# Twelve unread matrix products ahead of the first attention steps of a one-core retention and feed-forward kernel

## The chip, the cores and the metric

The kernel runs on one core of one Trainium2 chip. The metric is device microseconds (us) of one execution. The three runs of the kernel before have a median of 849.66 us, from 848.78 to 849.99.

## The reference

A retention layer with a decaying state, and two feed-forward layers behind it:

```python
for t in range(S):                                   # B, H, S, D = 4, 8, 768, 64
    state = gamma * state + einsum('bhd,bhe->bhde', k[:, :, t], v[:, :, t])
    y[:, :, t] = scale * einsum('bhd,bhde->bhe', q[:, :, t], state)
x = y as (3072, 512)
h = x @ w_in                                         # 512 -> 1024
solu = h * softmax(h); ln = layernorm(solu) * g_ln
x = ln @ w_out                                       # 1024 -> 512
h = x @ w_in2                                        # 512 -> 2048
out = (h * cos(h)) @ w_out2                          # 2048 -> 512
```

## The kernel before, in words

The recurrence is cut into chunks of 64 positions. There are 24 **steps**: two pairs of batches (`NB2`) by 12 chunks (`NI`), each for 8 heads and two batches at once. Step n has two input transfers of 512 KB, called `kq` (keys and queries by head dimension) and `kv` (keys and values by position); `load_step` (L379) issues both on SP's queue. `load_step(0)` also issues the table of decays, `c_all`, on ACT's queue.

What a step does, engine by engine:

- TensorE, `score_pair` (L411, products at L413): 16 products of 64x64 into the PSUM tile `sc`, from the step's `kq`. Each fp32 product stands in the trace as two records, so 32 for a step.
- DVE, `masks` (L432, recorded at L359): `s` is `sc` times the mask `mg`, which POOL makes in `prep` (L390) from `c_all`.
- ACT and DVE, `prep` (recorded at L356 and L402): the step's keys are scaled in four pieces `in<-in,c_all`, once `kv` has come.
- TensorE, `step` (L437): the outputs `y` (`out_pair`, L426) from `s`, the input and, from the second chunk on, the state `st`; and the new state `S` (`state_pair`, L419) from the scaled keys. The two kinds are issued alternately.
- ACT copies `S` to `st`; DVE and ACT make `x`, `xh` and `xl` from `y`. `xh` + `xl` are the two halves of the fp32 value in the fp32r format.

The first feed-forward layer's products are at L601 (`mm1`, L593): three 128x512 products for each weight piece and tile, `xh` by `w1h`, `xl` by `w1h`, `xh` by `w1l`, into the PSUM tiles `hA` and `hB`. The weights come as 512 KB transfers (L493) and are converted on ACT and DVE. After `mm1` come `norm`, the transposes (`transp`, L646), the second product (`mm2`, L670), and later the second feed-forward layer (`up`, L837, and `down`, L870), which ends the kernel.

The order of the work is not that of the code. Each piece of work is given to a planner, `P.add` (L83), with its engine, an assumed time, and what it reads and writes. `P.order` (L128) plays all engines with these assumed times and puts out one order for each. For TensorE it looks at the first ten pieces not yet placed (`WINDOW`, L65) and takes the one that can begin first, with 0.05 us against a piece for each place that it stands further back (L192 to L199):

```python
for k, i in enumerate(pe[:self.WINDOW]):
    if need[i] == 0:
        t = max(free[e], ready_at[i])
        c.append((max(free[e], ready_at[i] + self.MARGIN) + k * self.STEP, t, i))
```

A transfer can't land before `FIRST` (3.35, L69) in the planner's time, plus its own length, 128 / 16 * 4096 / 24.5e3 = 1.34 (L353), plus `LAND` (1.2, L61). TensorE is free from 0.7 on (L159). A piece on TensorE that waits only for other pieces on TensorE is ready as soon as they begin (L107, L241). What stands behind on an engine waits for what is ahead of it.

The code's order of the start (L962 to L985) is: transfers of steps 0 to 3 and of eight weight pieces in a fixed sequence; then, for n = 0, 1, 2, the scores of step n and the outputs and state of step n, where the scores of step 3 go with the outputs of step 2 (`attend()` without `False`); from L990 on the `mm1` products of tiles 0 to 2 are put between.

Of the kernel before, what the change touches and what calls it, by code (L numbers as in the profile page):

```python
# [27 lines left out]
NHP = H // 2  # L28
# [222 lines left out]
def body(ctx: ExitStack, tc: tile.TileContext, qkv, consts,  # L251
         w_in1, w_out1, w_in2, w_out2, out):
    nc = tc.nc
    ctx.enter_context(tc.manual_schedule())
    P = Plan()
# [31 lines left out]
    xls = [moe.tile([128, NHP, 128], F32R, name=f"xl{n}") for n in range(2)]  # L287
    xk = [(("xh", n), ("xl", n)) for n in range(2)]
# [9 lines left out]
    ys = moe.tile([128, 512], F32, name="ys")  # L298
# [4 lines left out]
    hB = psb.tile([128, 3, 512], F32, name="hB")  # L303
# [34 lines left out]

    HALF = ((slice(0, 64), slice(64, 128)), (slice(64, 128), slice(0, 64)))

    nc.gpsimd.memset(mhalf, -0.5)
    nc.gpsimd.memset(hp[:, 0:1], HALFPI)
    for t in tops:
# [11 lines left out]
    def act(out, in_, func, r, w, occ, lat=None, alt=None, **kw):  # L355
        return P.add("ACT", occ, lambda: nc.scalar.activation(out=out, in_=in_, func=func, **kw), r, w, lat, alt=alt)  # L356
# [18 lines left out]
    def ib(n):  # L375

        return n % NA if n < 2 * NA else (n - 2 * NA) % (NA - 1)
# [12 lines left out]
    def prep(n):  # L390
        i = steps[n][1]
        d = a_mg[n % 2]
        for u, m in enumerate((tri.unsqueeze(1).to_broadcast([128, NHP, C]), gat)):
            P.add("POOL", 0.6, lambda u=u, m=m: nc.gpsimd.tensor_tensor(  # L394
                out=d[:, u], in0=m, in1=cs[:, u, i].unsqueeze(2).to_broadcast([128, NHP, C]), op=ALU.mult),
                [("cs",)], [("amg", n % 2, u)], port=True)
        if has_state(n):
            k = a_kn[ib(n)]
            for a in range(NHP):
                f = cs[:, 2, i, a:a + 1]  # L400
                act(k[:, a], k[:, a], AF.Copy, [("cs",), ("in", ib(n), "kv")], [("ks", ib(n), a)], 0.295,
                    alt=("DVE", 0.2, lambda k=k[:, a], f=f: nc.vector.tensor_scalar(  # L402
                        out=k, in0=k, scalar1=f, scalar2=None, op0=ALU.mult), True), scale=f)

    def has_state(n):
        return steps[n][1] + 1 < NI
# [4 lines left out]
    def score_pair(n, j):  # L411
        for r, _ in HALF:
            nc.tensor.matmul(out=p_sc[r, j], lhsT=a_kt[ib(n)][r, j], rhs=a_q[ib(n)][r, j], start=True, stop=True)  # L413
# [14 lines left out]
    def scores(n):  # L428
        P.add("PE", 1.0, lambda: [score_pair(n, j) for j in range(8)], [("in", ib(n), "kq")], [("sc",)], lat=1.3)
        masks(n)  # L430

    def masks(n):  # L432
        tt(a_s[n % 2].rearrange("p (a b) t -> p a b t", b=2), p_sc.rearrange("p (a b) t -> p a b t", b=2),
           a_mg[n % 2][:, 0].unsqueeze(2).to_broadcast([128, NHP, 2, C]), ALU.mult,
           [("sc",), ("amg", n % 2, 0)], [("asc", n % 2)], occ=0.69)
# [175 lines left out]
    def norm(n):  # L611
        b = [hbank(n, c) for c in (0, 1)]
        h = h_of(n)
        hk = [b[0][1], b[1][1]]
        sm = sms[n % 3]
        smk = lambda *c: [("sm", n % 3, x) for x in c]
        u = us[n % UBUF]
        uk = [("u", n % UBUF, c) for c in (0, 1)]
        P.add("DVE", 1.135, lambda: nc.vector.tensor_reduce(  # L619
            out=sm[:, 0:1], in_=h, axis=AX.XY, op=ALU.max, negate=True), hk, smk(0))  # L620
        act(u, h, AF.Exp, hk + smk(0), uk + smk(1), 1.1, 1.35, bias=sm[:, 0:1], accum_out=sm[:, 1:2])
        stt(u, u, 1.0, h, ALU.mult, ALU.mult, hk, uk + smk(2), 1.18, accum_out=sm[:, 2:3])
        ts(sm[:, 3:4], sm[:, 2:3], -1.0 / FF1, None, ALU.mult, None, smk(2), smk(3), 0.07)
        act(junk, u, AF.Square, uk + smk(3), [("junk",)] + smk(4), 1.14, 1.38, bias=sm[:, 3:4], accum_out=sm[:, 4:5])
        ts(sm[:, 5:6], sm[:, 1:2], 1e-9, None, ALU.add, None, smk(1), smk(5), 0.07)
        stt(sm[:, 6:7], sm[:, 5:6], 1e-6, sm[:, 5:6], ALU.mult, ALU.mult, smk(5), smk(6), 0.07, port=True)
        stt(sm[:, 7:8], sm[:, 4:5], 1.0 / FF1, sm[:, 6:7], ALU.mult, ALU.add, smk(4, 6), smk(7), 0.07, port=True)
        P.add("POOL", 0.56, lambda: nc.gpsimd.tensor_tensor(out=sm[:, 8:9], in0=sm[:, 7:8], in1=mhalf, op=ALU.pow),
              smk(7), smk(8), port=True)
        tt(sm[:, 9:10], sm[:, 3:4], sm[:, 8:9], ALU.mult, smk(3, 8), smk(9), port=True, occ=0.07)  # L630
        act(u, u, AF.Identity, smk(8, 9), uk, 1.14,
            alt=("DVE", 0.75, lambda: nc.vector.tensor_scalar(
                out=u, in0=u, scalar1=sm[:, 8:9], scalar2=sm[:, 9:10], op0=ALU.mult, op1=ALU.add), True),
            scale=sm[:, 8:9], bias=sm[:, 9:10])
# [284 lines left out]
    def load_to(n):  # L919
        while loaded[0] <= min(n, ns - 1):  # L920
            load_step(loaded[0])
            loaded[0] += 1
# [6 lines left out]
    def weights(n):  # L929
        for _ in range(min(n, len(wq))):  # L930
            f, args = wq.pop(0)
            f(*args)
# [3 lines left out]
    def attend(ahead=True):  # L936
        n = nxt[0]
        if n >= ns:
            return
        nxt[0] += 1  # L940
        if n > 3:
            load_to(n + 1)
        if n + 1 < ns and ahead:
            prep(n + 1)
        step(n, ahead)
        if n == ns - 1:
            p2["sb_hook"] = [P.add("HOOK", 0.0, open_sb, lat=0.0, after=P.using({"in", "amg", "asc", "ast", "sc", "S", "y", "wt", "stg", "top"}))]
# [7 lines left out]
    def chunk(c, k, tiles=(0, 1)):  # L955
        for ms in ((0, 1), (2,)):
            for n in tiles:
                mm1(n, c, k, ms)
                if c == 0 and k == KD - 1 and 2 in ms:
                    norm(n)  # L960

    P.chained(True)  # L962
    load_to(0)
    act(sms[2][:, 0:1], mhalf, AF.Exp, (), [("sm", 2, 0)], 1.4)
# [9 lines left out]
    weights(1)  # L974
    weights(1)
    P.chained(False)
    prep(0)
    scores(0)
    attend(False)
    prep(1)  # L980
    scores(1)
    attend(False)
    prep(2)
    scores(2)
# [218 lines left out]
```

## Time and profile before

| what | before |
|---|---|
| runs, median (lowest to highest) | 849.66 us (848.78 to 849.99) |
| the profiled execution, its own time | 849.62 us |
| its span, first to last instruction | 847.9 us |
| TensorE busy in the span | 835.7 us |
| mean granted TensorE clock | 0.999 |

The profiled execution took 849.62 us, 1.72 us more than its span and 0.04 us less than the median of the runs. All rows further down are of this execution, in microseconds from the first instruction. TensorE's busy time is made of modelled ends of pipelined products, so starts are safer to read than durations. "Busy" of an engine that waits for nobody says nothing of what it would wait for if it came earlier: that has to be read from the times at which its inputs were there.

### The profile page before, as it was taken

Reading aid. Unit: us, or ns where it says so; the run is one execution under the profiler, and the core shown is the slowest. Engines: PE = TensorE matmul, PEld = TensorE weight load, DVE = VectorE, ACT = ScalarE, POOL = GpSimd, SP = SyncE. Lnnn points to the kernel's source line nnn. Section 1 sums busy time; section 2 is a strip of 40 time slices with the busy share of each in tenths; the row PEclk is TensorE's granted clock in tenths of the full one; section 3 lists DMA queues with packets and bytes.
Section 4 is the critical chain, followed back from the end, with each engine's and each line's share of the span. In section 5 each row is a group of like instructions: output and inputs, shape, how many; then the busy total and the mean of one; then the engine's idle time right before and its main releaser. Section 6 shows DMA issues by size and latency. Waiting matters only on the chain.

```text
span 847.9 us, 16467 instructions
## 1 busy us (share of the span) xinstructions
PE 835.7 (99%) x6448; PEld 692.6 (82%) x6448; DVE 614.1 (72%) x1113; ACT 467.3 (55%) x808; POOL 53.6 (6%) x85
## 2 busy tenths in 40 slices
PE   6999999999999999999999999999999999999997
PEld 6788888888888888888888888888888888888886
DVE  4899979877565573399888936878798277878820
ACT  4798867667543552376566614446474254645522
POOL 3122201111110010000000000000000000000000
PEclk9999999999999999999999999999999999999999
DMA  9991898998940143387556734755566365551442
GB/s 348 338 345 55 280 344 305 381 353 302 298 150 26 58 164 152 100 273 232 164 164 183 222 118 133 215 148 162 162 189 184 88 179 168 162 161 50 124 125 75
DMA packets 81053, 162.76 MB, mean 192 GB/s; under 512 B 8144, under 2 KB 22608, under 8 KB 80976
## 3 DMA queue, kind: packets, MB, share of 16 engines
q1 hardware_dynamic: 80512, 160.98, 58.7%
q8 instruction: 51, 0.84, 0.4%
q10 hardware_dynamic: 464, 0.73, 0.2%
q14 instruction: 26, 0.21, 0.1%
HBM read 117.64 MB, written 44.04 MB: 191 GB/s over the span
## 4 chain that ended last, share of the span: by engine, by line
PE 95%; DVE 2%; DMA 1%; ACT 1%; issue 0%; POOL 0%; ACTq 0%; DVEq 0%
PE acc L870 30%; PE U L837 26%; PE hA L601 13%; PE y L670 12%; PE y L426 5%; PE tr L670 3%; PE tr L646 2%; PE hB L601 2%; PE sc L413 1%; DMA c_all<-consts_dram 1%; PE S L419 1%; DMA raw<-y1d 0%; POOL mg L394 0%; DVE lt L657 0%; DVE s L359 0%
## 5 line engine op out<-in xcount | busy, mean ns | idle before, releaser
L870 PE MATMUL acc<-o2h,gh 128*128 128x512 f32 x384 | 149.4, 389 | 0.0
L870 PE MATMUL acc<-o2h,gl 128*128 128x512 f32 x384 | 149.4, 389 | 0.0
L870 PE MATMUL acc<-o2l,gh 128*128 128x512 f32 x384 | 149.4, 389 | 0.0
L670 PE MATMUL y<-lt,o1h 128*128 128x512 f32 x304 | 102.2, 399 | 0.0
L870 PEld LDWEIGHTS acc<-o2l,gh 128*128 128x128 f32 x384 | 72.1, 188 | 15.0
L870 PEld LDWEIGHTS acc<-o2h,gh 128*128 128x128 f32 x384 | 72.1, 188 | 14.9
L870 PEld LDWEIGHTS acc<-o2h,gl 128*128 128x128 f32 x384 | 72.1, 188 | 14.9
L801 DVE TENSOR_TENSOR gl<-gs,gh 128x512 fp32r<-128x512 f32 x48 | 33.1, 690 | 57.1 <-ACT gh L799 56.8
L799 ACT ACTIVATE gh<-gs 128x512 fp32r<-128x512 f32 x48 | 30.3, 631 | 70.7 <-PE acc L870 43.0
L670 PEld LDWEIGHTS y<-lt,o1h 128*128 128x128 f32 x304 | 57.1, 188 | 12.2
L601 PE MATMUL hA<-w1h,xh 128*128 128x512 f32 x160 | 64.7, 404 | 0.0
L601 PE MATMUL hA<-w1l,xh 128*128 128x512 f32 x160 | 62.6, 391 | 0.0
L601 PE MATMUL hA<-w1h,xl 128*128 128x512 f32 x160 | 62.4, 390 | 0.0
L670 PE MATMUL y<-lt,o1l 128*128 128x512 f32 x152 | 59.3, 390 | 0.0
L822 ACT ACTIVATE s<-U 128x512 f32<-128x512 f32 x72 | 42.4, 590 | 27.4 <-PE U L837 27.2
L787 ACT ACTIVATE ra<-ra,hp 128x512 f32<-128x512 f32 x48 | 34.6, 721 | 30.1 <-DVE ra L785 30.0
L426 PE MATMUL y<-s,in 64*64 64x64 f32 x768 | 48.6, 230 | 1.7 <-DVE s L359 1.7
L426 PEld LDWEIGHTS y<-s,in 64*64 64x64 f32 x768 | 39.0, 141 | 11.9 <-issue 7.4
L657 DVE TENSOR_TENSOR lt<-tr,lt 128x512 fp32r<-128x512 f32 x48 | 31.5, 686 | 18.1 <-ACT lt L655 17.8
L426 PE MATMUL y<-in,st 64*64 64x64 f32 x704 | 43.9, 222 | 0.0
L619 DVE TENSOR_REDUCE sm<-hA 128x1 f32<-128x1024 f32 x21 | 25.7, 1223 | 22.9 <-PE hA L601 22.5
L828 DVE TENSOR_TENSOR ha<-s,U 128x512 f32<-128x512 f32 x36 | 24.7, 686 | 23.2 <-ACT s L822 12.8
(165 smaller groups left out, 1968.2 us busy)
## 6 DMA issues: line engine op xcount, KB each, us to landing
wr<-wd SPq DMA_DIRECT2D x168, 256.0 KB, 2.7
in<-qkv_dram SPq DMA_DIRECT2D x48, 512.0 KB, 6.5
gs<-gd SPq DMA_DIRECT2D x48, 256.0 KB, 2.7
raw<-w_in_dram SPq DMA_DIRECT2D x16, 511.8 KB, 6.9
raw<-w_out_dram SPq DMA_DIRECT2D x16, 511.8 KB, 6.8
wd<-st SPq DMA_DIRECT2D x14, 512.0 KB, 6.4
wd<-stx SPq DMA_DIRECT2D x14, 512.0 KB, 6.1
gd<-rb SPq DMA_DIRECT2D x27, 256.0 KB, 2.4
```

The source lines that it names most:

```text
L426: nc.tensor.matmul(out=p_y[o, j], lhsT=a[r, j], rhs=b[r, j], start=not part, stop=bool(part) or not later)
L601: nc.tensor.matmul(out=h, lhsT=a[:, k], rhs=w1[lo][k][c], start=(k + m == 0), stop=(k == KD - 1 and m == 2))
L619: P.add("DVE", 1.135, lambda: nc.vector.tensor_reduce(out=sm[:, 0:1], in_=h, axis=AX.XY, op=ALU.max, negate=True), hk, smk(0))
L657: P.add("DVE", 0.6, lambda: nc.vector.tensor_tensor(out=lts[j][:, 1], in0=trs[s], in1=lts[j][:, 0].bitcast(F32), op=ALU.subtract), [("hb", ...
L670: nc.tensor.matmul(out=y1(), lhsT=w[:, j, ds], rhs=lts[j][:, a], start=(j + m == 0), stop=(j == K1 - 1 and m == 2))
L787: P.add("ACT", 0.62, lambda: nc.scalar.activation(out=p2["r"][r], in_=p2["r"][r], func=AF.Sin, bias=hp[:, 0:1]), (), [("r", r)])
L799: P.add("ACT", 0.54, lambda: nc.scalar.activation(out=p2["gh"][g], in_=src(), func=AF.Copy), [key], [("gh", g)], after=p2["cos_hook"])
L801: P.add("DVE", 0.6, lambda: nc.vector.tensor_tensor(out=p2["gl"][g], in0=src(), in1=p2["gh"][g].bitcast(F32), op=ALU.subtract), [key, ("gh ...
L822: P.add("ACT", 0.5, lambda: nc.scalar.activation(out=p2["s"][i], in_=p2["U"][a], func=AF.Copy), [ka], [("s", i)], after=p2["cos_hook"])
L828: P.add("DVE", 0.6, lambda: nc.vector.tensor_tensor(out=p2["h"][k], in0=p2["s"][i], in1=p2["U"][u], op=ALU.add), [("s", i), ("ub", u)], [( ...
L837: nc.tensor.matmul(out=p2["U"][u], lhsT=p2["wr"][slot[p, s, m]][:, kk, lo], rhs=p2["x"][m][xl][:, kk], start=(kk + q == 0 and m in (0, 1, ...
L870: nc.tensor.matmul(out=p2["acc"][t], lhsT=p2[a][g][:, ts_], rhs=p2["o2"][j // 2][lo][:, j % 2], start=(j == 0 and m == 0), stop=(j == K2 - ...
```

## The change

DVE fills 128 columns of `ys` with ones and copies them into `xls[1]` in the fp32r format, at the start. A new function `warm(n)` gives the planner n products of 128x128 by 128x512 of this constant, into the bank `hB[:, 2]`. Nothing reads what they write; the next writers of that bank are the `mm1` products of tile 2. `warm(8)` stands ahead of the scores of step 0, `warm(2)` between the scores and the outputs of step 0, and again of step 1.

```diff
+    nc.vector.memset(ys[:, 0:128], 1.0)
+    nc.vector.tensor_copy(xls[1][:, 0], ys[:, 0:128])
     nc.gpsimd.memset(mhalf, -0.5)
...
+    def warm(n):
+
+        for _ in range(n):
+            P.add("PE", 0.2267, lambda: nc.tensor.matmul(
+                out=hB[:, 2], lhsT=xls[1][:, 0], rhs=xls[1][:, 0:1].to_broadcast([128, NHP, 128]), start=True, stop=True),
+                [xk[1][1]], [("hB", 2)], lat=0.45)
...
     P.chained(False)
+    warm(8)
     prep(0)
     scores(0)
+    warm(2)
     attend(False)
     prep(1)
     scores(1)
+    warm(2)
     attend(False)
     prep(2)
     scores(2)
```

## Rows read from the trace of the kernel before

**Rows 1.** The page, part 1: busy time, share of span, records by engine.

```profile
PE 835.7 (99%) x6448; PEld 692.6 (82%) x6448; DVE 614.1 (72%) x1113; ACT 467.3 (55%) x808; POOL 53.6 (6%) x85
```

**Rows 2.** Waits of TensorE, 0 to 60 us: total, times, longest.

```profile
PE sc L413 <- DMA in<-qkv_dram: 5.5, 1, 5.5
PE y L426 <- DVE s L359: 1.7, 2, 0.9
PE hB L601 <- DVE u L367: 0.4, 1, 0.4
```

**Rows 3.** TensorE by stretch: stretch, length, busy (records), granted clock, DMA share, GB/s.

```profile
5.50:17.40 11.90, 10.21 (x252) 1.00 1.02 403
17.50:36.80 19.30, 19.30 (x328) 1.00 0.95 368
39.30:843.60 804.30, 804.06 (x5748) 1.00 0.58 185
843.60:846.80 3.20, 0.00 (x0) 1.00 0.30 84
846.90:847.90 1.00, 0.00 (x0) 0.50 0.00 0
```

**Rows 4.** Timeline of TensorE, 0 to 40 us: start, length, [idle before].

```profile
5.53 1.97 PE L413 MATMUL sc<-in 64*64 64x64 f32 x32 [5.53 <-DMA in<-qkv_dram]
...
9.06 0.32 PE L426 MATMUL y<-s,in 64*64 64x64 f32 x2
...
9.17 0.32 PE L426 MATMUL y<-s,in 64*64 64x64 f32 x2
...
10.14 1.92 PE L413 MATMUL sc<-in 64*64 64x64 f32 x32
12.85 0.37 PE L426 MATMUL y<-s,in 64*64 64x64 f32 x2 [0.79 <-DVE s L359]
...
17.65 0.50 PE L601 MATMUL hB<-w1h,xh 128*128 128x512 f32 x1
17.99 0.39 PE L601 MATMUL hB<-w1h,xl 128*128 128x512 f32 x1
18.22 0.39 PE L601 MATMUL hB<-w1l,xh 128*128 128x512 f32 x1
...
19.01 0.27 PE L426 MATMUL y<-s,in 64*64 64x64 f32 x2
...
19.29 0.23 PE L426 MATMUL y<-s,in 64*64 64x64 f32 x2
...
19.35 0.22 PE L426 MATMUL y<-s,in 64*64 64x64 f32 x2
...
21.95 0.27 PE L413 MATMUL sc<-in 64*64 64x64 f32 x2
```

**Rows 5.** Line 413 on TensorE, 17.42 to 17.6 us: ns min/median/max.

```profile
L413 PE MATMUL sc<-in x10: 218/252/311, 17.1 to 17.5; 64*64 64x64 f32 x10
```

**Rows 6.** Timeline of DVE, 7 to 48 us: start, length, [idle before].

```profile
7.62 0.69 DVE L359 TENSOR_TENSOR s<-sc,mg 128x512 f32<-128x512 f32 x1 [7.62 <-POOL mg L394]
8.23 0.86 DVE L402 TENSOR_SCALAR in<-in,c_all 128x128 f32<-128x128 f32 x2
...
17.86 0.68 DVE L359 TENSOR_TENSOR s<-sc,mg 128x512 f32<-128x512 f32 x1
```

**Rows 7.** Timeline of SP's queue, 0 to 60 us: start, length, issues.

```profile
4.31 1.52 SPq L384 DMA_DIRECT2D in<-qkv_dram  x2
```

**Rows 8.** DMA issues from 4.2 to 4.5 us: KB each, us to landing.

```profile
in<-qkv_dram SPq DMA_DIRECT2D x1, 512.0 KB, 10.8
```

**Rows 9.** DMA issues from 8.7 to 8.9 us.

```profile
in<-qkv_dram SPq DMA_DIRECT2D x1, 512.0 KB, 11.3
```

**Rows 10.** DMA issues from 3.6 to 3.7 us.

```profile
big<-w_in_dram SPq DMA_DIRECT2D x1, 511.8 KB, 8.8
```

**Rows 11.** DMA queues from 12.9 to 13.0 us: packets, MB, share of engines.

```profile
q8 instruction: 1, 0.02, 59.3%
```

## The prediction

> **What bounds the kernel now.** I read the page first: TensorE is busy for 835.7 of 847.9 us, no other engine for more than 72% [rows 1]. So the time is TensorE's work plus the little time in which it does none, and a change can give only what it takes from one or the other. The waits of TensorE in the first 60 us come to 7.6 us: 5.5 for the first input, 1.7 in two waits for the masked scores `s` of steps 0 and 1, 0.4 later [rows 2]. Then I cut the span into stretches. From 39.30 us to the last product TensorE is busy for 804.06 of 804.30 us, and from 17.5 to 36.8 for all of the time [rows 3]. Behind 39 us, then, the kernel moves as one piece: what is won or lost ahead of it arrives at the end, unless an input holds it.
>
> The third view is the pace of one kind of work in the timeline. In step 0, `y` and `S` records come in fours, and from one pair of `y` to the next it is 0.11 us (9.06 to 9.17). In step 2 the same pattern takes 0.06 us (19.29 to 19.35) [rows 4]. The records of line 413 go from 311 ns to 218 ns at about 17.4 us [rows 5]. [...] Ahead of the rise lie 10.21 us of busy time in 11.90 [rows 3], with waits of about 0.9 and, ahead of 12.85, 0.79 us in it [rows 2, 4]; TensorE had gone without a wait from 12.85 to 17.4, 4.6 us, when the clock rose.
>
> **The change, part by part.** *DVE, two operations.* DVE has nothing to do until 7.62 [rows 6]. One of its operations on 128x128 fp32 takes 0.43 us (two in 0.86) [rows 6]; two of them, begun where SP's and ACT's first work begins, at about 0.8, end at about 1.7. Cost on the path: nothing, covered by DVE's empty 7.62 us; without that cover it would be 0.9 us once. Who writes `xls[1]`, `ys` and the bank `hB[:, 2]` next does so after 12 us, so no new wait there.
>
> *Where the twelve products go.* The code puts two ahead of the outputs of step 0 and two ahead of step 1, but the planner need not. A product waits only for the one before it on TensorE, so it is ready at once; the scores of step 0 wait for their transfer, in the planner's time 3.35 + 1.34 + 1.2 = 5.9. Eight products of 0.2267 from 0.7 end at 2.5 there. The next two then stand at place 1, a penalty of 0.05 us, the last two at place 3, 0.15 us, all inside the window of ten: I expect all twelve in a row at the start, done at 3.4 in the planner's time, which is ahead of 5.9. So the rest of the order should stay as it is, on all engines, and SP's and POOL's queues too.
>
> *The twelve products.* A 128x512 product takes 0.23 us at the higher level (17.99 to 18.22) [rows 4] and, by the two paces, 0.23 * 0.11 / 0.06 = 0.42 at the lower. From 1.7 on, twelve last 2.8 us at best (end 4.5) and 5.0 at worst (end 6.7). The input is there at 5.5 [rows 4], so they delay the scores of step 0 by 0 to 1.2 us. If I take the one rise that this trace has, behind 4.6 us without a wait, it comes at about 6.3: eleven products are done, the last ends at 6.5, and the delay is 1.0.
>
> *What runs faster.* Scores of step 0: records in 0.96 instead of 1.92 us [rows 4], end about 7.6, as before (7.5). `s` ends at 8.3, as before [rows 6]. Step 0's outputs would take 1.0 instead of 1.8, but the last two key pieces are scaled on DVE behind `s`, until 9.1 [rows 6], so they end at about 9.6. Then the scores of step 1 to 10.6; `x`, the scaling and `s` of step 1 on DVE, 0.69 + 0.86 + 0.69, to about 11.9; outputs of step 1, which took from 12.85 to 16.2, halved, to about 13.7.
>
> *Where it stops.* The scores of step 2 come next in TensorE's order, and their transfer was issued at 4.31 and took 10.8 us [rows 7, 8]: it lands at 15.1, whatever TensorE does. The 16 DMA engines are full all that time (share 1.02) [rows 3]. So TensorE waits from 13.7 to 15.1, and most of what the clock gave is lost there: what was a late engine becomes a late input. From 15.15 the scores of step 2 take 1.0, and the five `mm1` products behind them 1.36 as before (17.65 to 19.01, already at the higher level) [rows 4]: the outputs of step 2 begin at 17.5 instead of 19.01. Their `s` is no later: scores' end 16.3, `s` 17.0, though it is at 17.86 now [rows 6]. **Gain: 1.5 us.** The order in which things move matters little: with a rise as late as 12 us, the outputs of step 1 would still be done by about 15.1, and the sum would be the same. Both ends for the unknown answer of the clock: if it does not rise earlier at all, the delay of up to 1.2 us stands alone, a loss; if no input held TensorE, see the first rival.
>
> *Behind it.* TensorE is full to 36.8, so the 1.5 us pass on if the other inputs allow it. The nearest is that of step 3, issued at 8.77 and landing 11.3 us later, 20.1 [rows 9]; it is needed at 21.95 [rows 4], then at 20.45: 0.4 us to spare. The waits for `s` of steps 0 and 1 remain.
>
> **Sum.** The profiled execution took 849.62 us, 0.04 less than the median of the runs. 849.62 - 1.5 = **848.1 us**, 0.18% less. About 0.2%, 1.7 us, is what a measurement of this kernel can tell from no change, so the forecast sits just inside it.
>
> **Rivals.** *First, the input of step 2 does not hold it: faster.* If all 10.2 us of slow work ran at the double pace, with a delay of 1.0, it would be 10.2 / 2 - 1.0 = 4.1 us: 845.5. For a smaller form of this: the weight piece issued at about 3.65 took 8.8 us [rows 10] and landed at 12.4, so the next transfer is 2.7 us behind it, though 512 KB at 403 GB/s [rows 3] need 1.3. If the 1.4 us between were an accident of this execution, the gain would be 2.9 and the time 846.7. Against both: an instruction transfer stood among the packets at 12.9 to 13.0 [rows 11], and TensorE's instructions have to be fetched in the changed kernel as well; and nothing in the planner's order puts other work ahead of the scores of step 2. Chance 0.18.
>
> *Second, the clock falls back in the new wait: slower.* The place is 13.7 to 15.1, TensorE idle for 1.4 us behind two shorter waits. At the end of the span the clock is still 1.00 in 3.2 us without a product, and 0.50 behind that [rows 3]; that speaks against a fall within 1.4 us. If it fell, the scores of step 2 would take 1.8 and the five products 2.5, and the outputs of step 2 would begin at 19.4, still slow until 15.15 + 4.6 = 19.7, which costs 0.2 more: 0.6 us late, 850.2. It decides where the wait is long enough to drop the level and the rise takes as long as before. The same happens a little earlier if constant products don't raise the clock at all: 849.6 + 1.2 = 850.8. Chance of both 0.15.
>
> [...]
>
> *Third, the planner's order changes elsewhere,* since the added pieces raise the ranks of what feeds the first steps; a wait of a us either way. Chance 0.05.
>
> **How the numbers follow.** Forecast 0.62, first rival 0.18, second 0.15, third 0.05. The forecast's own range is 847.5 to 848.8 (the clock's rise between 5 and 12 us, the landing within some 0.3 us, the spread of the runs); a quarter of it lies past 0.2%. Faster: 0.16 + 0.17 + 0.02 = 0.35. Slower by over 0.2%, past 851.3: 0.03 from the second and 0.01 from the third rival. Same: 0.61. The range takes in the smaller form of the first rival and the first form of the second: 846.6 to 850.2; outside stay the 4.1 us and the 850.8.
>
> **What would show it.** Twelve 128x512 products in a row from about 1.7 us, at 0.42 us and, if the rise falls into them, 0.23 at the end; the 311 ns records of line 413 gone by step 1; a new wait of TensorE at about 15 us for `in<-qkv_dram`; the outputs of step 2 at 17.5 and all later work 1.5 us earlier. The prediction is wrong if pairs of products stand between scores and outputs (then the planner was misread, though they would fit the 0.9 and 0.79 us waits), if the 15 us wait is missing, or if records of line 413 behind 15 us are at 311 ns again.

## The result, and the profile after

The kernel after takes **853.90 us** (median of six runs, 852.69 to 855.53) against 849.76 of the kernel before beside it: ratio 1.0054, interval 1.0044 to 1.0064. It is slower by 0.5%; the forecast was 848.1, and the whole range up to 850.2 lies below the result. The profiled execution took 854.77 us with a span of 853.0, so the traces differ by 5.1 us of span, of which the medians confirm some 4.1.

The page of the kernel after, parts 1 and 3 (TensorE's line answers to [rows 1]; queue, packets, MB, share):

```profile
PE 839.5 (98%) x6460; PEld 693.5 (81%) x6460; DVE 614.8 (72%) x1115; ACT 469.1 (55%) x808; POOL 54.3 (6%) x85
...
q8 instruction: 51, 0.84, 0.4%
```

Twelve more products, two more DVE operations, and nothing else added. The instruction queue's line becomes important below: 51 packets of 0.84 MB together are 16 KB each. TensorE has 6460 product records and 6460 weight loads, 12,920 in all, or 253 for each packet.

The waits of TensorE in the first 60 us, kernel after (total, times, longest), answer to [rows 2]:

```profile
PE y L428 <- issue: 2.5, 2, 1.3
PE y L428 <- DVE s L361: 2.1, 2, 1.2
PE hA L603 <- issue: 2.0, 1, 2.0
PE hB L967 <- DVE xl L342: 1.5, 1, 1.5
PE sc L415 <- issue: 0.5, 1, 0.5
...
```

The wait for the first input is gone (the products fill it). The waits for `s` stand as expected. New are four waits of 5.0 us together with the releaser "issue": nothing that the profile knows, no semaphore, transfer or other engine, ended them. The kernel before has none.

The timeline of TensorE, kernel after (start, length, idle before), answers to [rows 4]:

```profile
1.52 5.49 PE L967 MATMUL hB<-xl 128*128 128x512 f32 x12 [1.52 <-DVE xl L342]
6.94 1.15 PE L415 MATMUL sc<-in 64*64 64x64 f32 x32
8.96 0.27 PE L428 MATMUL y<-s,in 64*64 64x64 f32 x2 [0.87 <-DVE s L361]
12.34 0.27 PE L428 MATMUL y<-s,in 64*64 64x64 f32 x2 [1.23 <-DVE s L361]
15.19 0.21 PE L428 MATMUL y<-s,in 64*64 64x64 f32 x1 [1.13 <-issue]
21.88 0.27 PE L415 MATMUL sc<-in 64*64 64x64 f32 x1 [0.48 <-issue]
27.97 0.21 PE L428 MATMUL y<-in,st 64*64 64x64 f32 x1 [1.35 <-issue]
40.92 0.50 PE L603 MATMUL hB<-w1h,o1h 128*128 128x512 f32 x1 [0.44 <-DVE u L369]
50.01 0.40 PE L603 MATMUL hA<-w1l,o1h 128*128 128x512 f32 x1 [2.01 <-issue]
```

The scores of step 0 end at 8.1 and take 1.15 us instead of 1.97, and the `y` of steps 0 and 1 begin with records of 0.27 instead of 0.37: the clock rose at about 6.9. The trace's records of the granted clock agree. The first, at 1.00, begins at 6.90 in after and at 17.41 in before; ahead of it there is none, and the views print 1.00 for that time as well. The waits that follow stand in the middle of `y`, in front of scores, again in `y`, and in the middle of an `mm1` product: at places that have nothing in common in the code.

TensorE by stretch, kernel after (stretch, length, busy, granted clock, DMA share, GB/s), behind the last of them:

```profile
51.28:54.67 3.39, 3.39 (x10) 0.50 1.01 403
54.70:58.00 3.30, 3.30 (x15) 1.00 1.02 416
```

Behind the wait of 2.0 us the clock falls, from 51.27 to 54.68: 10 records in 3.39 us at 0.50, where the starts of 128x512 products are 0.42 to 0.43 us apart, and 15 in 3.30 at 1.00, where they are 0.23 apart. The sum: the product that waits for `u` stands at the same place in the order of every kernel here, and serves as a fixed point. It comes at 40.92 instead of 39.30, 1.6 late; the wait at 50 adds 2.0; 3.39 us at half the pace cost 1.7. That is 5.3, beside 5.1 in the spans. And of the waits for "issue" 3.0 us lie ahead of 40.92: without them, if nothing else held TensorE in their place, the fixed point would be at 37.9, 1.4 us *earlier* than before. By this subtraction the forecast's 1.5 us were won, and lost again on the way.

What sets the places of the four waits shows when records are counted. All engines by stretch, kernel after, from the start to the end of each wait (stretch, length, then busy time and records of TensorE's products, of its weight loads, DVE, ACT, POOL, then clock, DMA share, that is the mean busy share of the core's 16 DMA engines, and GB/s):

```profile
0.00:15.19 15.19, 10.45 (x222) 8.41 (x223) 6.29 (x12) 6.45 (x13) 6.95 (x20) 1.00 0.85 326
0.00:21.88 21.88, 16.63 (x350) 12.90 (x350) 11.51 (x22) 10.77 (x20) 8.55 (x22) 1.00 0.91 354
0.00:27.96 27.96, 21.37 (x477) 16.71 (x478) 16.46 (x29) 14.28 (x27) 9.77 (x24) 1.00 0.93 368
0.00:50.01 50.01, 40.97 (x860) 32.60 (x861) 35.47 (x69) 31.80 (x63) 14.02 (x31) 1.00 0.86 326
```

Products and loads together: 445, 700, 955, 1721. The steps are 255, 255 and 766, one more than three times 255. A packet of 16 KB for each 255 records is 64 bytes a record. If one instruction in some 256 leaves no busy record, the author's estimate from these counts, each wait stands where a block of 256 instructions, one packet, ends. Where the next block was, the queue's packets tell. DMA queues of the kernel after, from 12.8 to 12.9 us and from 47.6 to 47.7:

```profile
q8 instruction: 1, 0.02, 58.4%
...
q8 instruction: 1, 0.02, 59.8%
```

A packet is under way from 12.81, 19.55, 25.51 and 47.69, for about 0.9 us each, and the waits end 2.3 to 2.5 us after each start. Both sides fit: TensorE seems to wait for the next 16 KB of its program. The page lists these packets beside those of the weights and inputs, as shares of the same 16 DMA engines: 0.4% of the span for the instruction queue and 58.2% for the largest of the others. From the end of the first wait to that of the second (15.19 to 21.88) one such packet starts, at 19.55, and from there to that of the third (27.97) one, at 25.51: these waits give no sign that blocks lay ready further ahead than the next.

How long the next packet takes to start can be read behind each end of a block. Of the kernel after, from TensorE's first record in a block to the start of the next packet, at 445 and at 1976 records (all engines by stretch):

```profile
15.19:19.55 4.36, 4.33 (x116) 3.34 (x116) 3.63 (x7) 2.55 (x6) 1.61 (x2) 1.00 1.03 420
62.12:62.68 0.56, 0.56 (x52) 0.56 (x48) 0.56 (x3) 0.56 (x2) 0.30 (x1) 1.00 0.07 29
```

It is 4.36 us at a DMA share of 1.03, and 0.56 us at 0.07.

From there the theory: the **supply theory** says that the 24 records (12 products, 12 loads) at the front move each block's end 24 records up in the work. Behind scores and `y`, where eight records take 0.06 us [rows 4], that is hardly earlier; behind `mm1`, where two take 0.23 us [rows 4], the next block is needed up to 12 x 0.23 = 2.8 us earlier, and isn't there. The rival, the **clock theory**, says that the loss comes with the earlier clock, wherever the blocks end: TensorE uses up its program faster than it comes.

### The profile page after: what moved, and what is told of

It is laid out like the page before. It is cut to its first block, busy times and chain, and to the rows that moved or that the text cites. A ratio compares the mean times of both kernels' runs of the same rounds, so it can differ in the third digit from the quotient of the medians.

```text
span 853.0 us, 16493 instructions
## 1 busy us (share of the span) xinstructions
PE 839.5 (98%) x6460; PEld 693.5 (81%) x6460; DVE 614.8 (72%) x1115; ACT 469.1 (55%) x808; POOL 54.3 (6%) x85
## 3 DMA queue, kind: packets, MB, share of 16 engines
q1 hardware_dynamic: 80512, 160.98, 58.2%
## 4 chain that ended last, share of the span: by engine, by line
PE 97%; DVE 1%; issue 1%; DMA 0%; ACT 0%; DVEq 0%
PE acc L872 31%; PE U L839 27%; PE hA L603 13%; PE y L672 12%; PE y L428 4%; PE tr L672 3%; PE tr L648 2%; PE hB L603 2%; PE sc L415 1%; PE hB L967 1%; PE S L421 1%; DMA raw<-y1d 0%; DVE lt L659 0%; DVE s L361 0%; DVE sm L621 0%
## 5 line engine op out<-in xcount | busy, mean ns | idle before, releaser
L872 PEld LDWEIGHTS acc<-o2l,gh 128*128 128x128 f32 x384 | 72.1, 188 | 15.1
L428 PE MATMUL y<-s,in 64*64 64x64 f32 x768 | 46.6, 222 | 3.2 <-DVE s L361 2.1
L428 PEld LDWEIGHTS y<-s,in 64*64 64x64 f32 x768 | 37.3, 134 | 13.6 <-issue 8.7
L830 DVE TENSOR_TENSOR ha<-s,U 128x512 f32<-128x512 f32 x36 | 24.7, 686 | 23.1 <-ACT s L824 12.8
```

The source lines that it names most:

```text
L428: nc.tensor.matmul(out=p_y[o, j], lhsT=a[r, j], rhs=b[r, j], start=not part, stop=bool(part) or not later)
L830: P.add("DVE", 0.6, lambda: nc.vector.tensor_tensor(out=p2["h"][k], in0=p2["s"][i], in1=p2["U"][u], op=ALU.add), [("s", i), ("ub", u)], [( ...
L872: nc.tensor.matmul(out=p2["acc"][t], lhsT=p2[a][g][:, ts_], rhs=p2["o2"][j // 2][lo][:, j % 2], start=(j == 0 and m == 0), stop=(j == K2 - ...
```

## The experiments

In the diffs below the lines of the change itself are not repeated, and `...` marks lines left out. The median of the kernel before beside the runs is 849.5 to 849.6.

**Records or clock: tiny12.** The twelve products, all in one place, with four columns instead of 512: the same records, hardly any work.

```diff
...
-                out=hB[:, 2], lhsT=xls[1][:, 0], rhs=xls[1][:, 0:1].to_broadcast([128, NHP, 128]), start=True, stop=True),
+                out=hB[:, 2, 0:4], lhsT=xls[1][:, 0], rhs=xls[1][:, 0, 0:4], start=True, stop=True),
...
-    warm(8)
+    warm(12)
...
```

> Twelve products of 128x128 by 128x4 at the start in place of twelve by 128x512: the same 24 TensorE records more than before, but TensorE busy for about 1 us instead of 5. Supply theory (TensorE's instructions come in packets of 16 KB, 256 instructions each, asked for as it goes and late while the 16 DMA engines are full, so it stands still where it reaches a packet's first instruction too early): the clock rises at about 17.4 us as before, TensorE reaches the packets' first instructions a little earlier than before because they lie 24 records further up, so some of the waits of the changed kernel return, smaller: 850.5 to 852.5 us. Clock theory (the loss comes from TensorE at the higher level running ahead of the other engines in the first 17 us, whatever the number of records): no loss, 849.3 to 850.2 us.

853.23 us, ratio 1.0044 (1.0032 to 1.0057). The timeline of TensorE, tiny12:

```profile
12.97 0.32 PE L428 MATMUL y<-s,in 64*64 64x64 f32 x2
...
28.06 0.21 PE L428 MATMUL y<-in,st 64*64 64x64 f32 x1 [1.22 <-issue]
...
49.83 0.40 PE L603 MATMUL hA<-w1l,o1h 128*128 128x512 f32 x1 [1.74 <-issue]
```

At 12.97 the records still take 0.32 us, the pace of before: by it the clock did not come early, and the loss is there all the same. The clock theory falls as the cause of this loss. The two waits stand in front of the operations of the third and fourth wait of after, at the same counts (tiny12, all engines by stretch):

```profile
0.00:28.05 28.05, 22.25 (x477) 19.21 (x478) 16.55 (x29) 14.11 (x27) 9.76 (x24) 1.00 0.94 364
0.00:49.83 49.83, 41.85 (x860) 35.10 (x861) 35.34 (x67) 31.36 (x61) 14.01 (x31) 1.00 0.88 330
```

**More records: heat32 and heat112.** 32 products with 192 columns, then 112 with 64 rows and columns, all at the start in place of the twelve, to move the ends of the blocks further.

```diff
...
-    warm(8)
+    warm(32)
...
-                out=hB[:, 2], lhsT=xls[1][:, 0], rhs=xls[1][:, 0:1].to_broadcast([128, NHP, 128]), start=True, stop=True),
+                out=hB[:, 2, 0:192], lhsT=xls[1][:, 0], rhs=xls[1][:, 0:1, 0:48].to_broadcast([128, NHP, 48]), start=True, stop=True),
```

```diff
...
-    warm(8)
+    warm(112)
...
-                out=hB[:, 2], lhsT=xls[1][:, 0], rhs=xls[1][:, 0:1].to_broadcast([128, NHP, 128]), start=True, stop=True),
+                out=hB[0:64, 2, 0:64], lhsT=xls[1][:, 0, 0:64], rhs=xls[1][:, 0, 0:64], start=True, stop=True),
```

> 32 products of 128x128 by 128x192 at the start in place of twelve by 128x512: TensorE busy as long (12 x 512 = 32 x 192 columns), clock up at the same time, but 64 records more than before instead of 24. Supply theory: the waits stand at the same record numbers of TensorE as in the changed kernel (the 449th, 705th, 961st and so on, 256 apart), thus in front of other operations, and cost more since these fall into denser parts: 855 to 859 us. Clock theory, and any theory in which the waits belong to the operations (a semaphore that the profile does not show): the waits stand ahead of the same operations as in the changed kernel, and the time is the same, 853 to 855 us.

> 112 products of 128x64 by 128x64 at the start in place of twelve by 128x512: TensorE busy for about 6 us, 224 records more than before. Supply theory: the packets' first instructions now fall 32 records further down than before the change (224 - 256), into parts that TensorE reaches late anyway, and the first packet is asked for during the scores of step 0: nearly no waits, the gain of the clock stays, 847.9 to 849.7 us, faster than the changed kernel by 4 us or more. Clock theory: as the changed kernel or later, 853.5 to 855.5 us.

heat32: 853.62 us, ratio 1.0043 (1.0030 to 1.0055). The time is below what the supply theory gave and inside the rival's range; the places decide, and they are the supply theory's. TensorE's timeline and the counts of heat32 (all engines by stretch):

```profile
16.57 0.26 PE L421 MATMUL S<-in 64*64 64x64 f32 x1 [2.20 <-issue]
22.49 0.27 PE L428 MATMUL y<-in,st 64*64 64x64 f32 x2 [0.19 <-issue]
```

```profile
0.00:16.57 16.57, 10.20 (x222) 9.68 (x223) 6.84 (x12) 5.87 (x11) 6.86 (x20) 1.00 0.89 334
0.00:22.48 22.48, 15.92 (x350) 14.66 (x350) 10.66 (x19) 8.91 (x17) 8.47 (x22) 0.92 0.92 356
```

Other operations than in after (a state product, and `y` where scores stood), the same 445 and 700 records from the start. The place of the wait goes with the count, not with the work. Behind the 2.20 us the granted clock was 0.50 for 3.3 us (16.60 to 19.90).

heat112: 858.33 us, 1.0109 (1.0095 to 1.0123). That is far above the expectation. The time says nothing on the theories, since I had costed its products wrongly. Its timeline has them in one row:

```profile
1.52 12.15 PE L967 MATMUL hB<-xl 128*64 128x64 f32 x112 [1.52 <-DVE xl L342]
```

0.11 us each, so the scores of step 0 begin at 13.6, eight us late. Its waits for "issue" in the first 60 us, of 0.56 and 0.82 us, stand at 701 and 956 records.

**Less traffic: lowdma.** After, with weight pieces 5 to 8 transferring 32 bytes of each row; the conversions read another piece's words. It leaves out half of the first layer's first weights.

```diff
+        w = 17 if 4 <= n < 8 else 2048
+        into = raw
+        if 4 <= n < 8:
+            raw = big[n - 4]
-        dma(lambda: eng.dma_start(out=raw.bitcast(I16)[:, 0:2047], in_=src[:, 1:2048]), (128, 4096), w=rk,
+        dma(lambda: eng.dma_start(out=into.bitcast(I16)[:, 0:w - 1], in_=src[:, 1:w]), (128, 4096), w=rk,
```

> The changed kernel, where the transfers of the fifth to the eighth weight piece of the first layer move 32 bytes of each row instead of 4 KB, and another piece's words are converted in their place (so the first layer's second half of weights is left out, and 2 MB of the transfers of the first 27 us). Supply theory: the DMA engines are empty earlier, from about 22 us, so the packet ahead of the wait at 28 us comes in time: that wait (1.35 us) goes, the two earlier ones stay, and the time falls by 1 to 3 us against the changed kernel, 851 to 853 us. Clock theory: the waits do not depend on the DMA engines, 853 to 855 us, or the one at 28 us stays.

853.38 us, 1.0053 (1.0037 to 1.0070): as after. That lies above the supply theory's 851 to 853 and in the rival's range. The timeline of TensorE, lowdma:

```profile
26.70 0.21 PE L428 MATMUL y<-in,st 64*64 64x64 f32 x1 [0.46 <-issue]
...
48.95 0.39 PE L607 MATMUL hA<-w1l,o1h 128*128 128x512 f32 x1 [2.20 <-issue]
```

The wait in `y`, inside the lightened time, fell from 1.35 to 0.46; the one near 15 stayed, as expected, and so did the one near 49, outside of the lightened time. The shorter wait is for the supply theory, but the time does not carry it.

**The program moved, and nothing else: before_p24.** The kernel before, with a placing order at its start, by which TensorE's program stands 24 instructions further on in its block; the filled place is jumped over. No product is added.

```diff
+    nc.tensor.addr_align(256, offset=89, max_nops=0)
```

> The kernel before, with nothing added that computes: TensorE's program is only placed 24 instructions further on against the 256-instruction blocks in which it is fetched (a directive ahead of the first instruction that fills the place in front and jumps over it). Supply theory: the boundaries of the blocks fall on the same operations as in the changed kernel, so its waits come back although there is no product and no earlier clock: waits near the 28 and 49 us marks, 852.5 to 854 us, as with the twelve 4-column products (853.2). Rival (the loss comes from the products being there, in DVE's or TensorE's order or in the bank they write): 849.0 to 850.2 us.

853.63 us, 1.0051 (1.0038 to 1.0063): the whole loss, without the change. Timeline of TensorE, before_p24:

```profile
27.85 0.21 PE L427 MATMUL y<-in,st 64*64 64x64 f32 x1 [1.40 <-issue]
...
49.39 0.39 PE L602 MATMUL hA<-w1l,o1h 128*128 128x512 f32 x1 [1.47 <-issue]
```

Its other waits in the first 60 us are those of [rows 2]; the two new ones stand in front of the same operations as in after. The counts of before_p24, and of the kernel before at the count of after's last wait (all engines by stretch):

```profile
0.00:27.84 27.84, 19.19 (x465) 16.37 (x466) 15.78 (x27) 14.10 (x27) 9.66 (x24) 1.00 0.93 364
0.00:49.38 49.38, 38.84 (x848) 32.26 (x849) 34.30 (x64) 31.04 (x61) 13.91 (x31) 1.00 0.87 330
```

```profile
0.00:48.94 48.94, 41.31 (x860) 34.94 (x861) 35.47 (x68) 32.16 (x64) 14.48 (x33) 1.00 0.91 337
```

931 and 1697: 24 fewer than in after, since the 24 are here an empty place instead of products. In before, count 1721 is reached at 48.94, twelve `mm1` products further in the work, without a wait. This run decides between the theories.

**Moved the other way, and the change put back in place: before_m32, after_p0, after_m32.**

```diff
+    nc.tensor.addr_align(256, offset=33, max_nops=0)
```

is before_m32, the kernel before 32 instructions further up. After_p0 is after with `offset=41`, which puts the ends of the blocks on the operations where they fell before; after_m32 has `offset=9`, again 32 less.

> The kernel before, its TensorE program placed 32 instructions nearer to the start of a block than before (the boundaries come 32 instructions later in it). Supply theory: no wait appears and there was hardly one to remove, 848.8 to 849.8 us. Rival: 849.0 to 850.2 us; the two do not differ here, the run says whether the kernel before itself had something to gain from its place.

> The changed kernel with all twelve products, its TensorE program placed so that the boundaries of the blocks fall on the operations on which they fell before the change. Supply theory: the waits at 28 and 50 us go, a wait of about half a us may stay near 15 us, and the loss goes with them: 848.3 to 849.8 us, 4 us faster than the changed kernel. Rival (the products or the earlier clock do it): 853 to 855 us as the changed kernel.

> The changed kernel, its TensorE program placed so that the boundaries of the blocks come 32 instructions later in the work than before the change. Supply theory: later boundaries leave the first ones more time, so this should give the most of what the clock can give, 847.9 to 849.3 us. Rival: 853 to 855 us as the changed kernel.

**After_p0: 849.66 us, 1.0003 (0.9994 to 1.0012).** All twelve products are there, and the loss is gone. Its waits of TensorE:

```profile
...
PE y L429 <- issue: 1.2, 1, 1.2
...
```

The waits near 22, 28 and 50 don't stand any more; one of 1.2 us at 15.65 does, and it takes most of what the earlier clock gave.

Before_m32 (851.05 us, 1.0020, 1.0012 to 1.0029) and after_m32 (850.59, 1.0010, 1.0001 to 1.0018) missed: both came out above the expectation. The waits of before_m32 name why:

```profile
PE sc L414 <- DMA in<-qkv_dram: 6.7, 1, 6.7
...
PE y L427 <- issue: 0.7, 1, 0.7
PE sc L414 <- issue: 0.7, 1, 0.7
```

The first input comes some 1.2 us later than in before (TensorE waits 6.7 us for it instead of 5.5; an instruction packet is under way at 2.9 us, where before has none; that the filled place ends in another block is the author's estimate), and two ends of blocks came to places where 0.7 us is waited. Moving further is not better; each place has its own waits.

**The control, and the change in the traffic: before_p0, before_low, p24_low.** Before_p0 is the kernel before with the placing order at the place where it stands anyhow (`offset=65`). The other two are the places 65 and 89 with the weight pieces of the first layer from the fifth on at 32 bytes a row; they leave out half of its first weights and all of its second, and DVE zeros four of the tiles at the start.

```diff
...
+    for n in range(4, 8):
+        nc.vector.memset(big[n], 0)
...
+        w = 17 if 4 <= n < 16 else 2048
-        dma(lambda: eng.dma_start(out=raw.bitcast(I16)[:, 0:2047], in_=src[:, 1:2048]), (128, 4096), w=rk,
+        dma(lambda: eng.dma_start(out=raw.bitcast(I16)[:, 0:w - 1], in_=src[:, 1:w]), (128, 4096), w=rk,
```

> The kernel before with the placing directive, set so that TensorE's program lies as it did without it: a control for the directive itself. Both theories: 849.0 to 850.2 us, no waits of TensorE without a releaser; if the directive costs something of its own, for instance a late first input, it shows here.

> The control with less DMA traffic: the fifth to the sixteenth weight transfer of the first layer (four of its first matrix, all eight of its second) move 32 bytes of each row instead of 4 KB, 6 MB less in the first 50 us; DVE fills four of the tiles with zeros at the start. So half of the first layer's first weights and all of its second weights are left out. The base for the next run: about 848.5 to 850 us, no waits of TensorE without a releaser.

> The run before it with the program placed 24 instructions further on, as in before_p24, and the same weights left out. If the packets of instructions come late because the DMA engines are full (supply theory with its cause): the waits at 28 and 49 us go or shrink below 0.5 us, and the time is that of before_low within 0.8 us, where full traffic gave 4.0 us between the two placings. If a packet takes the same time whatever else moves (a fixed latency of the fetch): the waits stay and the difference is 3 to 4 us again.

Before_p0: 849.77 us, 1.0001 (0.9992 to 1.0010): the order itself costs nothing, and 65 fits the natural place: 65 + 445 records is 510, two short of the end of a second block. Before_low: 849.56 (0.9997, 0.9988 to 1.0005). P24_low: 850.20 (1.0008, 1.0000 to 1.0017). With the full traffic the 24 places cost 853.63 - 849.77 = 3.9 us, with the lighter one 850.20 - 849.56 = 0.6. TensorE does the same work in both pairs, so what the move costs depends on the traffic. Not each wait went with the traffic: before_low, for which none was expected, has two (waits of TensorE, before_low):

```profile
PE hB L605 <- issue: 1.4, 1, 1.4
PE y L429 <- issue: 0.6, 1, 0.6
```

They end at 29.13 and 15.40. Of p24_low's expectation, too, half failed: the wait in `y` stayed (1.33 us at 26.5). The DMA engines are then still full: a share of 0.96 to 1.06 in the stretches from 19 to 28 us, where inputs move. The one near 49 is gone; p24_low, TensorE by stretch:

```profile
46.00:49.70 3.70, 3.70 (x17) 1.00 0.85 254
```

Busy throughout, at a DMA share of 0.85.

Before_p0 brought what I had not looked for. Lines of TensorE by form, 12 to 14 us (ns min/median/max), of before_p0 and of the kernel before:

```profile
L427 PE MATMUL y<-s,in x24: 217/219/268, 12.6 to 13.9; 64*64 64x64 f32 x24
```

```profile
L426 PE MATMUL y<-s,in x12: 311/311/366, 12.9 to 13.9; 64*64 64x64 f32 x12
```

The same work, and in this execution the clock rose by itself, by the pace at about 11 us: the last 22 score records of step 1 take 1.00 us from 10.74, where in before the last 20 take 1.28 from 10.78. Then the waits of before_p0:

```profile
PE y L427 <- issue: 1.4, 2, 0.7
...
PE hB L602 <- issue: 0.3, 1, 0.3
```

They end at 15.40, 22.22 and 28.86, at 445, 700 and 955 records, where the kernel before, slower until 17.4, has none. So the pace has its share after all. In these executions an early clock with the blocks in the old place brings waits near 15 and 22 (before_p0; in after_p0 the first alone) and about makes up for them (849.77 and 849.66 us). The moved blocks with a late clock bring the waits near 28 and 50 (tiny12, before_p24), and nothing makes up for those (853.23 and 853.63). After has all four.

**Fewer products: heat8.** After without the two pairs: eight products, 16 records, in front.

```diff
...
-    warm(2)
...
-    warm(2)
...
```

> The changed kernel with the first eight products alone, 16 instructions more than before instead of 24. Supply theory: the waits at 28 and 50 us shrink by the time in which TensorE takes 8 instructions there, a few tenths of a us to 1 us each: 850.5 to 853 us. Rival (a fixed price of having products at all): 853 to 855 us.

850.67 us, 1.0023 (1.0011 to 1.0035). Waits of TensorE, heat8:

```profile
PE hA L603 <- issue: 1.1, 1, 1.1
PE S L421 <- issue: 1.1, 1, 1.1
PE y L428 <- issue: 0.9, 1, 0.9
```

Again at 445, 955 and 1721 records, on other operations. The first of these ends at 13.97 us, where before reaches 445 records at 16.00, and the fixed point behind `u` came at 38.70, 0.6 ahead of before; the wait in `hA` took that back. With eight products, too, the change loses.

## Why the prediction was wrong

The fixed point puts the four cases together. "Rest" is its time less the waits for "issue" ahead of it, less the 39.30 of before; each is one profiled execution.

| kernel | behind `u` at | issue waits until there | rest | median |
|---|---|---|---|---|
| after | 40.92 | 3.0 | -1.4 | 853.90 |
| after_p0 | 38.78 | 1.2 | -1.7 | 849.66 |
| before_p24 | 40.84 | 1.4 | +0.1 | 853.63 |
| before_p0 | 39.87 | 1.7 | -1.1 | 849.77 |

- *DVE's two operations, the twelve in a row.* Right: the order of all engines is the one of before, apart from the twelve at the front and DVE's two. They begin at 1.52, stand 0.42 to 0.43 us apart from the second on, and the last ends at about 7.0 (forecast 6.5). The scores of step 0 come at 6.94 instead of 5.53, 1.4 us late, more than the 1.2 of the worst case.
- *The clock.* Right: it rose at about 6.9 (forecast 6.3), and what followed ran at the higher level up to the fall at 51.27. The 1.00 of [rows 3] ahead of 17.4 stands where the trace has no clock record, so that the early pace is a lower level is an inference. What the runs show is the pace: 128x512 products 0.42 to 0.43 us apart ahead of 6.9, as behind 51.27 at the granted clock 0.50, and 0.23 at 1.00.
- *What runs faster.* Right for the scores of step 0, 1.15 us. The outputs of step 1 were under way at 12.34 at the higher level, and then stopped.
- *Where it stops.* **This is the step that failed.** It named the next input, landing at 15.1, as all that could hold TensorE. What held it, by the counts, is its own program, in the wait that ends at 15.19, at 445 records and 2.4 us behind the start of a packet. That this wait falls nearly where the forecast had one, 13.7 to 15.1, is chance: it stands inside the outputs of step 1, and the input is there. The transfer of step 2 was early: the DMA issues of after from 4.2 to 4.5 us, beside [rows 8], show

```profile
in<-qkv_dram SPq DMA_DIRECT2D x1, 512.0 KB, 9.4
```

  which, issued at 4.16, is a landing at 13.6. The first rival's smaller form was right about that transfer, and gained nothing by it.
- *Behind it.* "The 1.5 us pass on if the other inputs allow it" counted inputs alone. They were won (rest -1.4) and given to four waits, and the fourth, at 50, lies in the time that I called one piece.
- *Both ends for the unknown.* A delay of at most 1.2 us was the worst that I allowed; the added records had no price of their own. [Rows 11] showed an instruction packet amid the transfers, and the text said that instructions "have to be fetched in the changed kernel as well", but I used it as a delay of a transfer and never asked who waits for the packet itself. How much room there was can be read in the kernel before (all engines by stretch):

```profile
0.00:16.00 16.00, 8.81 (x221) 8.44 (x224) 5.84 (x10) 6.72 (x13) 6.87 (x20) 1.00 0.88 325
```

  It reaches 445 records at 16.0, 3.1 us behind the start of the packet of [rows 11], at 12.95. Of these, 2.3 to 2.5 pass until a waiting TensorE goes on, so some 0.7 us were to spare, an estimate. Count 445 falls near the end of step 1's outputs, and the forecast had these done at 13.7 instead of 16.2, far more than the room.
- *Second rival.* The fall of the clock came, 1.7 us worth, but behind a 2.0 us wait at 50, not at 14. That [rows 3] show 3.2 us without a fall was no protection.

**What is shown and what is not.** Shown: the loss comes with the place of the program (before_p24, 853.63 us), goes with it (after_p0, 849.66), stands on counts of 255 to 256 records, and shrinks with the traffic (p24_low against before_low, 0.6 us instead of 3.9). That a block is asked for when the one before it is entered is only inferred: from a block's end to the next packet's start it was 4.4 us (15.19 to 19.55) and 3.6 (21.88 to 25.51) at a DMA share of 1.02 to 1.03, and 0.56 at 0.07 (62.12 to 62.68). But full engines alone don't set it, for in before it was 2.7 us (16.00 to 18.66), at a share of 1.05. Open is why the clock fell behind the waits of 2.0 us in after and 2.2 in heat32, but not behind the 2.2 in lowdma. That the earlier clock would pay 1.1 to 1.7 us, were the program always in time, is worked out in the table and wasn't tried; no version here beats the kernel before.

## What to carry to other kernels

Here TensorE's program behaved as one more input while the DMA engines were full (a mean share of 0.85 to 0.93 up to the four waits of after, of 0.5 to 2.0 us). So count the instructions that a change puts ahead, and look at the operations on which the ends of the 256-instruction blocks then fall. What pointed to it were waits "for issue" 255 records or three times that apart, each ending 2.3 to 2.5 us behind the start of an instruction packet (after). A small change of a tuned kernel should be compared with the same change in its old place, since moving the program alone was worth 0.5% here.

## What the runs showed of the hardware that was not expected

- The same program 24 instructions further on costs 4 us of 850 (before_p24), more than all that the change was to win.
- The clock's rise is no property of the program alone: it came at 17.41 us in the execution of before and, by the pace, at about 11 in that of before_p0, which does the same work at the same place.
- 112 products of 64 columns in a row for 12.15 us did not bring the faster pace: in heat112 the 32 score records behind them took 1.97 us, as in before, and the `y` records that follow still 0.32.
- A wait of 2.0 us was followed by 3.4 us at the granted clock 0.50, though in [rows 3] the clock is 1.00 through 3.2 us without a product.
